# A fused attention and feed-forward kernel: the weight conversion split between VectorE and GpSimd, the score scale moved into the maximum pass, turned rows copied plainly

## The chip, the cores and the metric

The kernel runs on one core of one Trainium2 chip. A core has five engines that run their own instruction streams and meet through semaphores: TensorE (PE in the profile; its weight loads are PEld), VectorE (DVE), ScalarE (ACT), GpSimd (POOL) and SyncE (SP, which here only issues DMAs). The metric is the device time of one execution in microseconds (us). Three runs of the kernel before took 1281.09, 1281.25 and 1282.95 us; the median is 1281.25.

## The reference

```python
def _attn_ref(q, k, v, tau):                 # 8 batches, 8 heads, 576 rows, 64 columns
    scale = 1.0 / np.sqrt(q.shape[-1])
    scores = scale * np.matmul(q, k.transpose(0, 1, 3, 2))
    thresh = np.max(scores, axis=-1, keepdims=True) - tau
    scores = np.where(scores >= thresh, scores, -1000000000.0)
    scores = scores - np.max(scores, axis=-1, keepdims=True)
    attn = np.exp(scores)
    attn = attn / (np.sum(attn, axis=-1, keepdims=True) + 1e-09)
    return np.matmul(attn, v).astype(np.float32)

def _moe_ref(x, w_in, w_out):                # x 4608 x 512, w_in 512 x 2048, w_out 2048 x 512
    h = np.maximum(x @ w_in, 0.0)
    return (h * h @ w_out).astype(np.float32)
```

The attention output, with its heads side by side, is the input `x` of the feed-forward part. `w_in` and `w_out` arrive as 64-bit floats (they are scaled by a 64-bit scalar), everything else as 32-bit floats. The kernel computes in 32-bit floats.

## The kernel before

The kernel has two parts, one after the other. The feed-forward part multiplies with fewer products of sub-blocks than the plain way would take, and needs sums and differences of blocks of the weights and of `x`. The attention part runs first, and in its shadow the weights are fetched, converted to 32 bits and summed. The change touches the attention part alone.

**Periods.** The 64 heads are taken in 32 pairs; the rows of two pairs make nine units of 128 score rows, 144 units in all. The attention part is a loop over periods (`period`, line 631), each of which scores two units, A and B, turns the attention weights of units that were scored before, and multiplies those with the values. In what order each period issues its steps is written out by hand as lists of step names: `FIRSTS` for periods 0 to 2, `CONVERTING` (line 609) for the periods in which a chunk of weights is converted, 3 to 34, and `PLAIN` (line 606) for the rest, 35 to 71. Each engine carries out its own steps in the order in which they are issued.

The steps of a period that matter here, with their engines:

- `SA`, `SB` (PE): the scores of A and B into PSUM, for the two heads of a pair. q and k have been turned before, so that the head's columns lie on partitions: `T` (PE) turns them into PSUM, `eT` (ACT) takes them out, into `qT`, `kT` and `qR`. `qR` holds the 64 last rows of q of a pair, which are turned together with k. In eight of nine periods one q or one k is turned, in turns. `eT` also multiplies q by `qscale`, which is minus one eighth, by an activation with a per-partition scale (`scaled`, line 412); so the scores come out negative and scaled, and the row maximum becomes a minimum.
- `topA0`, `topA1`, `topB0`, `topB1` (DVE, line 463): a pass over the scores in PSUM which copies them to SBUF and takes each row's minimum along the way. It multiplies by the constant 1.0.
- `leastA`, `leastB` (POOL, line 470): the minimum plus tau, the threshold.
- `powA0` to `powB1` (ACT, line 473): the exponential.
- `maskA0` to `maskB1` (DVE, line 478): one instruction which compares the scores with the threshold, multiplies by the exponential and sums the row. It reads scores and exponentials from SBUF, and the threshold as a per-partition operand.
- `over` (POOL, line 485), `inv` (DVE, line 488), `spread` (POOL, line 528): one over the row sums, spread over 256 columns.
- `U`, `V`, `W` (PE, line 388) and `eU`, `eV`, `eW` (ACT, line 535): the attention weights (and the spread factors) turned, and copied to `wT`.
- `PV` (PE, line 544): the values times the weights, into two banks of PSUM. `x`: these come out into SBUF, one bank by DVE, which multiplies by the turned factors on the way (line 665), one by a plain copy on ACT (line 667). `xs` (POOL, line 682): that copy times its factors, 128 columns. Then SP writes `x` to DRAM.

**The conversion** takes one chunk of 128 x 512 64-bit floats at a time; a chunk arrives as pairs of 32-bit words, low word first, so each half is addressed as every second word (`pick`). `c1` (ACT, line 208) takes the high words without their sign into `a`; `c3` (POOL, line 221) clamps them to the range of 32-bit floats; `c4` (DVE, line 229) shifts `a` left by three and cuts it to 30 bits; `c2` (ACT, line 214) scales the low words down to the three bits that count; `c5` (DVE, line 237) keeps the two upper bits of the high words and joins `a` to them, in one instruction; `c6` (POOL, line 248) adds high and low words as integers, into the weight's place (chunks 0 to 15) or into `a`, from where it goes to DRAM. In `CONVERTING` the steps c3 to c6 of a chunk run in the period behind its c1 and c2, and stand in this order on their engines: DVE topA1, topA0, topB0, topB1, c4, inv, maskA1, x, maskA0, maskB0, c5, maskB1; POOL c3, over, leastA, leastB, spread, c6, xs; ACT c1, eU, powA1, powA0, powB0, eT, x, powB1, eV, eW, c2.

In the plain periods POOL makes one of the sums of weight blocks per period (`s1`, from line 582), and the order on DVE is topA1, topA0, topB1, inv, topB0, maskA1, maskA0, x, maskB1, maskB0.

Of the kernel before, what the change touches and what calls it, by code (L numbers as in the profile page):

```python
# [10 lines left out]
FP32 = mybir.dt.float32  # L11
# [37 lines left out]
def kernel(  # L49
# [183 lines left out]
    def convert5(m):  # L233
        if m not in parts:
            return
        lo, hi, a = parts[m]
        nc.vector.scalar_tensor_tensor(
            out=hi, in0=hi, scalar=-(1 << 30), in1=a, op0=ALU.bitwise_and, op1=ALU.bitwise_or
        )

    def convert6(m):
# [3 lines left out]
        raws.pop(m)  # L245
        if m < 16:
            a = weight(m)[:, :].bitcast(I32)
# [90 lines left out]
    def places(i):  # L338
        if i not in turned:
            turned[i] = (  # L340
                sb.tile([P, MAIN], FP32, tag="qT", bufs=Q_RING, name="qT"),
                sb.tile([P, S], FP32, tag="kT", bufs=K_RING, name="kT"),
                sb.tile([P, REST], FP32, tag="qR", bufs=K_RING, name="qR"),
            )
# [54 lines left out]
    def turn(i, which, spots, other=None):  # L399
# [8 lines left out]
        half = FULL * HALF  # L408

        kind = "turned k" if which else "turned q"  # L410

        def scaled(to, spot):
            touch(kind, nc.scalar.activation(out=to, in_=spot[0], func=AF.Identity, scale=qscale[:, :]), spot[1], BANK, i)

        def then():
            part = lambda r, x, n: (spots[r][0][:, ds(x, n)], spots[r][1])
            if which:
                for r, n in ((0, half), (1, half + REST)):
                    spot = part(r, 0, n)
                    copy_by = other if r and other else nc.scalar.copy  # L420
                    touch(kind, copy_by(to[1][:, ds(r * half, n)], spot[0]), spot[1], BANK, i)
                scaled(to[2], part(0, half, REST))
                next_keys(i)
            else:
                for r in range(2):
                    scaled(to[0][:, ds(r * half, half)], part(r, 0, half))
                for n in later_loads(i, 0):
                    load_q(n)
# [5 lines left out]
    def scores(n, rest):  # L434

        of, t = units[n]
        at_k, count = (MAIN, REST) if rest else (0, MAIN)
# [917 lines left out]
```

## Time and profile before

The profiled execution spans 1278.6 us from the first to the last instruction, 2.65 us under the median of the runs, with the TensorE clock granted in full throughout.

| engine | busy us in the span | share |
|---|---|---|
| PE matmul | 1255.2 | 98% |
| PE weight load | 1087.0 | 85% |
| DVE | 1000.2 | 78% |
| ACT | 855.6 | 67% |
| POOL | 897.4 | 70% |

The attention part ends at about 486 us (the last `inv` starts at 485.84); the integer sums of the conversion start at 35.15 (the first) to 252.12 (the last); from there to the end of the attention part the periods are plain. In the feed-forward part PE is busy without a gap.

How to read the lines: a line of the timeline gives the start in us from the span's start, the duration, the engine, the line of the kernel, the operation, what it writes and reads by the program's names, and the shapes. All tiles in SBUF are parts of one buffer called `arena`; the weights lie in `wall`; `sc` and `pt` are in PSUM. In brackets stands the idle time of the engine ahead of the instruction, and what ended it, as far as it can be inferred. Instructions of one engine overlap at their ends, as the next is started while the last results are written; so what an instruction costs its engine is the time from its start to the next one's start. A line of the windows gives for each engine the busy time within a stretch, and the number of instructions.

### The profile page before, as it was taken

What the parts mean: (1) busy time and instruction counts of PE and PEld (TensorE: products, weight loads), DVE (VectorE), ACT (ScalarE), POOL (GpSimd) and SP (SyncE); (2) the same over time, 40 slices, a digit from 0 to 9 for tenths busy, and PEclk for the clock granted to TensorE, in tenths of its full rate; (3) what the DMA queues carried; (4) which work ended last, traced back from release to release, by engine and by line L of the source; (5) the groups of instructions that cost most, each with busy time, mean ns of one, the idle gap of its engine ahead of it and who ended that gap; (6) DMA issues with size and microseconds to landing.
All of it is one profiled execution on the core that took longest, in us unless ns stands there. A gap on an engine that the chain in (4) does not pass through costs nothing.

```text
span 1278.6 us, 44201 instructions
## 1 busy us (share of the span) xinstructions
PE 1255.2 (98%) x17459; PEld 1087.0 (85%) x17459; DVE 1000.2 (78%) x2449; ACT 855.6 (67%) x1552; POOL 897.4 (70%) x1094
## 2 busy tenths in 40 slices
PE   8999999999999999999999999999999999999998
PEld 6666666677777768988888888999999999999998
DVE  6999999999999997787878877877645664565463
ACT  6999999999999995666765767667422441343240
POOL 2565665655555557888798889858877777786775
PEclk9999999999999999999999999999999999999999
DMA  6566666544333413457666666589635414522511
GB/s 155 152 158 160 165 193 182 151 94 112 89 83 84 97 34 98 156 164 219 198 190 204 192 198 187 177 324 394 208 122 166 133 50 149 166 95 76 161 35 34
DMA packets 256591, 191.89 MB, mean 150 GB/s; under 512 B 96000, under 2 KB 217344, under 8 KB 256384
## 3 DMA queue, kind: packets, MB, share of 16 engines
q1 hardware_dynamic: 254928, 188.63, 49.8%
q8 instruction: 137, 2.24, 0.7%
q14 instruction: 70, 0.57, 0.1%
q10 hardware_dynamic: 1456, 0.44, 0.1%
HBM read 116.65 MB, written 72.35 MB: 148 GB/s over the span
## 4 chain that ended last, share of the span: by engine, by line
PE 70%; DMA 1%; ACT 1%; DVE 1%; issue 1%; ACTq 0%; DVEq 0%; SPq 0%
PE po L1085 30%; PE ph L946 27%; PE sc L544 5%; PE sc L445 4%; PE pt L388 2%; DMA wall<-w 1%; PE sc L406 1%; PE sc L388 1%; DVE arena L128 1%; DVE arena L463 0%; DMA g<-arena 0%; ACT arena L916 0%; ACT c L879 0%; DMA arena<-xT 0%; ACT arena L917 0%
## 5 line engine op out<-in xcount | busy, mean ns | idle before, releaser
L128 POOL TENSOR_TENSOR arena<-arena 128x512 f32<-128x512 f32 (+1 forms) x314 | 377.7, 1222 | 126.3 <-DVE arena L128 89.4
L1085 PE MATMUL po<-wall,arena 128*128 128x128 f32 x3528 | 394.4, 275 | 0.2 <-DVE arena L125 0.2
L1085 PEld LDWEIGHTS po<-wall,arena 128*128 128x128 f32 x3528 | 394.1, 192 | 0.4 <-DVE arena L125 0.4
L946 PE MATMUL ph<-arena,wall 128*128 128x128 f32 (+1 forms) x2352 | 387.4, 327 | 1.1 <-DVE arena L665 0.5
L946 PEld LDWEIGHTS ph<-arena,wall 128*128 128x128 f32 x2352 | 354.2, 191 | 34.2 <-DVE arena L128 2.2
L128 DVE TENSOR_TENSOR arena<-ph,arena 128x512 f32<-128x512 f32 x378 | 255.6, 688 | 75.8 <-PE ph L946 50.0
L125 POOL TENSOR_TENSOR arena<-arena 128x128 f32<-128x128 f32 (+2 forms) x314 | 255.2, 814 | 29.1 <-DMA arena<-w 10.7
L879 ACT COPY c<-arena 128x512 f32<-128x512 f32 (+2 forms) x319 | 176.1, 558 | 104.2 <-DVE arena L125 85.7
L473 ACT ACTIVATE arena<-arena 128x576 f32<-128x576 f32 x288 | 232.1, 918 | 16.7 <-DVE arena L463 16.7
L128 DVE TENSOR_TENSOR arena<-po,arena 128x128 f32<-128x128 f32 x378 | 108.3, 290 | 168.0 <-PE po L1085 167.4
L478 DVE SCALAR_TENSOR_TENSOR arena<-arena 128x576 f32<-128x576 f32 x288 | 225.5, 811 | 0.4 <-POOL arena L470 0.4
L463 DVE TENSOR_SCALAR_CACHE_REDUCE arena<-sc 128x576 f32<-128x576 f32 x288 | 204.5, 751 | 14.3 <-ACT arena L535 6.4
L125 DVE TENSOR_TENSOR arena<-arena,c 128x512 f32<-128x512 f32 (+2 forms) x283 | 176.8, 633 | 7.9 <-ACT c L879 6.1
L544 PEld LDWEIGHTS sc<-arena 64*64 64x64 f32 x5760 | 144.4, 133 | 43.1 <-DVE arena L463 39.1
L445 PE MATMUL sc<-arena 64*64 64x64 f32 (+1 forms) x2304 | 170.0, 415 | 0.3 <-DVE arena L665 0.3
L544 PE MATMUL sc<-arena 64*64 64x128 f32 (+1 forms) x5760 | 160.8, 262 | 8.5 <-DVE arena L463 5.8
L535 ACT COPY arena<-pt 128x1024 f32<-128x1024 f32 x144 | 166.0, 1153 | 1.6 <-PE pt L388 1.5
L769 ACT COPY arena<-po 128x128 f32<-128x128 f32 x63 | 16.6, 264 | 185.4 <-PE po L1085 185.4
L388 PEld LDWEIGHTS pt<-ident,arena 64*128 64x128 f32 x2304 | 83.0, 138 | 41.7 <-ACT arena L535 33.8
L388 PE MATMUL pt<-ident,arena 64*128 64x64 f32 x2304 | 100.8, 227 | 2.4 <-ACT arena L535 2.1
L445 PEld LDWEIGHTS sc<-arena 64*64 64x64 f32 x2304 | 62.5, 132 | 47.5 <-issue 22.7
L470 POOL TENSOR_SCALAR arena<-arena,tau_p 128x2 f32<-128x2 f32 x144 | 65.5, 455 | 41.8 <-DVE arena L463 35.2
(51 smaller groups left out, 936.6 us busy)
## 6 DMA issues: line engine op xcount, KB each, us to landing
g<-arena SPq DMA_DIRECT2D x144, 256.0 KB, 2.6
arena<-g SPq DMA_DIRECT2D x144, 256.0 KB, 4.5
w<-arena SPq DMA_DIRECT2D x60, 256.0 KB, 2.8
wall<-w SPq DMA_DIRECT2D x49, 256.0 KB, 5.3
arena<-w SPq DMA_DIRECT2D x44, 256.0 KB, 3.1
arena<-in_v_dram SPq DMA_DIRECT2D x32, 288.0 KB, 4.6
out_dram<-arena SPq DMA_DIRECT2D x70, 128.0 KB, 2.4
arena<-in_q_dram SPq DMA_DIRECT2D x64, 128.0 KB, 4.1
```

Of the source, the lines that this page charges most:

```text
L125: e.tensor_tensor(out=out, in0=x, in1=y, op=ALU.subtract)
L128: e.tensor_tensor(out=out, in0=x, in1=y, op=ALU.add)
L388: made = nc.tensor.transpose(pt[:, r, ts(slot, HALF)], of[rows, :], ident[rows, rows])
L445: made = nc.tensor.matmul(sc[at, ds(to, count)], lhs, kT[rows, ds(at_k, count)], start=True, stop=True)
L463: made = nc.vector.tensor_scalar(out=s[:, j, :], in0=sc[:, ds(at, S)], scalar1=1.0, scalar2=None, op0=ALU.mult, op1=ALU.min, accum_out=nmx ...
L473: nc.scalar.activation(out=w[:, :, j, :], in_=of(j), func=AF.Exp, bias=nmx[:, j : j + 1], scale=-1.0)
L478: nc.vector.scalar_tensor_tensor(out=w[:, :, j, :], in0=of(j), scalar=thr[:, j : j + 1], in1=w[:, :, j, :], op0=ALU.is_le, op1=ALU.mult, a ...
L535: touch("weights", nc.scalar.copy(joined(to), whole(pt, 0, count)), at, 2 * BANK, m)
L544: made = nc.tensor.matmul(sc[ds(u * D, D), ds(5 * j * BANK + row, count)], loaded_v[i][rows, (c - (u != j)) % CH, :], wT[m][rows, ds(weigh ...
L879: nc.scalar.copy(c, y)
L946: nc.tensor.matmul(to[:, j, :], W_IN[m, k][:, ts(h * parts_ + j, P)], x_of(m, k), start=(not more and j == 0), stop=True, skip_group_check ...
L1085: nc.tensor.matmul(to, g[:, j, :], w[:, j, :], start=(not more and j == 0), stop=(j == 3), skip_group_check=True)
```

## The change

Four edits, all in the attention part.

1. **c5 and c6.** c5 only masks the high words (one input, one constant). c6 becomes two integer sums on POOL: low words plus `a`, in the low words' place, and then high words plus these, as before.
2. **The scale.** q is no longer scaled when it is taken out of PSUM. The pass over the scores multiplies by the per-partition operand `qscale` in place of the constant 1.0.
3. **Plain copies of turned rows.** As nothing is scaled on the way, both halves of a turned q come out by plain copies (2 of 256 columns, before 2 activations of 256), and those of a turned k by two copies of 320 columns, the last of which are the 64 rows of q or k (before: copies of 256 and 320 and an activation of 64). `kT` and `qR` become one tile of two halves of 320, in the same space; the scores read the 512 main keys as two runs of 256.
4. **x.** Both banks are copied by ACT, and xs on POOL multiplies all 256 columns in one instruction. DVE has no part in it.

```diff
@@ convert5, convert6
-        nc.vector.scalar_tensor_tensor(
-            out=hi, in0=hi, scalar=-(1 << 30), in1=a, op0=ALU.bitwise_and, op1=ALU.bitwise_or
-        )
+        nc.vector.tensor_scalar(out=hi, in0=hi, scalar1=-(1 << 30), scalar2=None, op0=ALU.bitwise_and)
...
         lo, hi, a = parts.pop(m)
         raws.pop(m)
+        nc.gpsimd.tensor_tensor(out=lo, in0=a, in1=lo, op=ALU.add)
         if m < 16:
             a = weight(m)[:, :].bitcast(I32)
         nc.gpsimd.tensor_tensor(out=a, in0=hi, in1=lo, op=ALU.add)
@@ places
-                sb.tile([P, MAIN], FP32, tag="qT", bufs=Q_RING, name="qT"),
-                sb.tile([P, S], FP32, tag="kT", bufs=K_RING, name="kT"),
-                sb.tile([P, REST], FP32, tag="qR", bufs=K_RING, name="qR"),
+                sb.tile([P, 2, FULL * HALF], FP32, tag="qT", bufs=Q_RING, name="qT"),
+                sb.tile([P, 2, (FULL + 1) * HALF], FP32, tag="kT", bufs=K_RING, name="kT"),
@@ turn
-        def scaled(to, spot):
-            touch(kind, nc.scalar.activation(out=to, in_=spot[0], func=AF.Identity, scale=qscale[:, :]), spot[1], BANK, i)
+        kind, n = "turned k" if which else "turned q", (FULL + (1 if which else 0)) * HALF
 
         def then():
-            part = lambda r, x, n: (spots[r][0][:, ds(x, n)], spots[r][1])
+            for r, copy_by in enumerate((nc.scalar.copy, other or nc.scalar.copy)):
+                touch(kind, copy_by(to[which][:, r, :], spots[r][0][:, 0:n]), spots[r][1], BANK, i)
             if which:
-                for r, n in ((0, half), (1, half + REST)):
-                    spot = part(r, 0, n)
-                    copy_by = other if r and other else nc.scalar.copy
-                    touch(kind, copy_by(to[1][:, ds(r * half, n)], spot[0]), spot[1], BANK, i)
-                scaled(to[2], part(0, half, REST))
                 next_keys(i)
             else:
-                for r in range(2):
-                    scaled(to[0][:, ds(r * half, half)], part(r, 0, half))
...
@@ scores
-                qT, kT, qR = turned[of[c]]
-                lhs = qT[rows, ds((c * FULL + t) * HALF, HALF)] if t < FULL else qR[rows, :]
-                made = nc.tensor.matmul(
-                    sc[at, ds(to, count)], lhs, kT[rows, ds(at_k, count)], start=True, stop=True
-                )
+                qT, kT = turned[of[c]]
+                lhs = qT[rows, c, ts(t, HALF)] if t < FULL else kT[rows, 0, ds(FULL * HALF, REST)]
+                keys = kT[rows, 1, ds(FULL * HALF, REST)] if rest else kT[rows, :, 0 : FULL * HALF]
+                to_ = sc[at, ds(to, count)] if rest else sc[at, ds(to, count)].rearrange("p (r n) -> p r n", r=2)
+                made = nc.tensor.matmul(to_, lhs, keys, start=True, stop=True)
@@ softmax, top
-                out=s[:, j, :], in0=sc[:, ds(at, S)], scalar1=1.0, scalar2=None,
+                out=s[:, j, :], in0=sc[:, ds(at, S)], scalar1=qscale[:, :], scalar2=None,
@@ period, given_out and scaled_x
-                by_vector = (0,)
                 for j in range(2):
-                    by = sc[:, ds(5 * j * BANK, P)], wT[m][:, ts(SCALE_AT + j, P)]
-                    if j in by_vector:
-                        made = nc.vector.tensor_tensor(out=x[:, j, :], in0=by[0], in1=by[1], op=ALU.mult)
-                    else:
-                        made = nc.scalar.copy(x[:, j, :], by[0])
-                    touch("x", made, 5 * j * BANK, P, m)
-                late["x"] = x, [j for j in range(2) if j not in by_vector], wT[m]
+                    touch("x", nc.scalar.copy(x[:, j, :], sc[:, ds(5 * j * BANK, P)]), 5 * j * BANK, P, m)
+                late["x"] = x, wT[m][:, ds(SCALE_AT * P, 2 * P)]
...
-                for j in js if len(js) == 1 else ():
-                    nc.gpsimd.tensor_tensor(out=x[:, j, :], in0=x[:, j, :], in1=by[:, ts(SCALE_AT + j, P)], op=ALU.mult)
+                x, by = late["x"]
+                flat = x[:, :, :].rearrange("p j q -> p (j q)")
+                nc.gpsimd.tensor_tensor(out=flat, in0=flat, in1=by, op=ALU.mult)
                 give_x(m, x)
```

More of the change, by code (lines that the diff above doesn't have):

```diff
@@ L407, in turn @@
                 touch("turns", made, at, BANK)
-        half = FULL * HALF
-        kind = "turned k" if which else "turned q"
-        def scaled(to, spot):
-            touch(kind, nc.scalar.activation(out=to, in_=spot[0], func=AF.Identity, scale=qscale[:, :]), spot[1], BANK, i)
+        kind, n = "turned k" if which else "turned q", (FULL + (1 if which else 0)) * HALF
         def then():
-            part = lambda r, x, n: (spots[r][0][:, ds(x, n)], spots[r][1])
+            for r, copy_by in enumerate((nc.scalar.copy, other or nc.scalar.copy)):
+                touch(kind, copy_by(to[which][:, r, :], spots[r][0][:, 0:n]), spots[r][1], BANK, i)
             if which:
-                for r, n in ((0, half), (1, half + REST)):
-                    spot = part(r, 0, n)
-                    copy_by = other if r and other else nc.scalar.copy
-                    touch(kind, copy_by(to[1][:, ds(r * half, n)], spot[0]), spot[1], BANK, i)
-                scaled(to[2], part(0, half, REST))
                 next_keys(i)
             else:
-                for r in range(2):
-                    scaled(to[0][:, ds(r * half, half)], part(r, 0, half))
-                for n in later_loads(i, 0):
-                    load_q(n)
+                for n_ in later_loads(i, 0):
+                    load_q(n_)
         return then
@@ L436, in scores @@
         of, t = units[n]
-        at_k, count = (MAIN, REST) if rest else (0, MAIN)
+        count = REST if rest else MAIN
         for j in range(2):
```

6 lines of the change are left out of this document (removed).

## The prediction

> **What bounds the kernel now.** I read first the busy time by stage, then the timelines of VectorE (DVE), GpSimd (POOL) and ScalarE (ACT) inside one attention period, because the shares of the whole span hide that the change touches attention alone. The two windows below run from the first to the last integer sum of the weight conversion (32 chunks, so 31 pitches) and over the plain periods behind it.
>
> ```profile
> core 0 of [0], span 1278.6 us
> core 0: us, PE busy (x) PEld busy (x) DVE busy (x) ACT busy (x) POOL busy (x), PEclk, DMA share, GB/s
> 35.15:252.12 216.97, 205.12 (x4952) 144.33 (x4952) 215.07 (x621) 216.72 (x380) 131.40 (x218) 1.00 0.64 167
> 261.00:477.00 216.00, 214.48 (x5530) 155.82 (x5526) 207.67 (x622) 205.86 (x349) 119.61 (x208) 1.00 0.37 85
> ```
>
> In the converting stage DVE (215.07 of 216.97) and ACT (216.72) are both full, PE is not; the pitch is 216.97/31 = 7.00 us. In the plain stage PE is full (214.48 of 216.00) and DVE has 4% left. POOL looks idle by 40% in both; the question is whether that idle time can be used.
>
> One converting period on DVE, from its first mask (line 478) to the next period's:
>
> ```profile
> 172.26 0.79 DVE L478 SCALAR_TENSOR_TENSOR arena<-arena 128x576 f32<-128x576 f32 x1
> 172.97 0.08 DVE L478 DVE_READ_ACCUMULATOR arena<-arena 128x1 f32 x1
> 172.97 0.28 DVE L665 TENSOR_TENSOR arena<-sc,arena 128x128 f32<-128x128 f32 x1
> 173.18 0.81 DVE L478 SCALAR_TENSOR_TENSOR arena<-arena 128x576 f32<-128x576 f32 x1
> ...
> 174.65 0.68 DVE L237 SCALAR_TENSOR_TENSOR arena<-arena 128x512 int32<-128x512 int32 x1
> 175.26 0.81 DVE L478 SCALAR_TENSOR_TENSOR arena<-arena 128x576 f32<-128x576 f32 x1
> 176.00 0.08 DVE L478 DVE_READ_ACCUMULATOR arena<-arena 128x1 f32 x1
> ...
> 178.71 0.42 DVE L229 TENSOR_SCALAR arena<-arena 128x512 int32<-128x512 int32 x1
> 179.04 0.17 DVE L488 RECIPROCAL arena<-arena 128x4 f32<-128x4 f32 x1
> 179.13 0.78 DVE L478 SCALAR_TENSOR_TENSOR arena<-arena 128x576 f32<-128x576 f32 x1
> ```
>
> Columns: start, duration, engine, line. Instructions overlap at their ends, so I count from start to start: a mask 0.74, the fused step c5 (line 237) 174.65 to 175.26 = 0.61, c4 (line 229) 178.71 to 179.04 = 0.33, the x product (line 665) 0.21. The period is 179.13 - 172.26 = 6.87 with no gap: this is DVE's own rate, and the 7.00 mean comes from other periods in which ACT is the slower one.
>
> POOL in the same stretch (in brackets the idle time ahead):
>
> ```profile
> 175.48 1.48 POOL L248 TENSOR_TENSOR arena<-arena 128x512 int32<-128x512 int32 x1 [2.17 <-ACT arena L535]
> 176.92 0.45 POOL L682 TENSOR_TENSOR arena<-arena 128x128 f32<-128x128 f32 x1
> ...
> 178.37 0.29 POOL L470 TENSOR_SCALAR arena<-arena,tau_p 128x2 f32<-128x2 f32 x1
> ```
>
> The sum of c6 starts 0.16 after c5 has ended, while the last mask (175.26 to 176.00) still runs. The 2.17 idle ahead of it lies exactly under the two middle masks and c5. That is the gap into which the new, second integer sum falls, and what such a neighbourhood costs is seen once in this trace, in an early period (DVE, then POOL):
>
> ```profile
> 26.99 0.82 DVE L478 SCALAR_TENSOR_TENSOR arena<-arena 128x576 f32<-128x576 f32 x1
> 27.73 0.08 DVE L478 DVE_READ_ACCUMULATOR arena<-arena 128x1 f32 x1
> 27.73 1.01 DVE L478 SCALAR_TENSOR_TENSOR arena<-arena 128x576 f32<-128x576 f32 x1
> 28.67 0.08 DVE L478 DVE_READ_ACCUMULATOR arena<-arena 128x1 f32 x1
> ```
> ```profile
> 27.19 0.93 POOL L682 TENSOR_TENSOR arena<-arena 128x128 f32<-128x128 f32 x1 [0.83 <-ACT arena L667]
> ```
>
> POOL's 128-wide sum comes at 27.19, inside a mask. It takes 0.93 instead of the 0.45 above: it waits for that mask's end at 27.73 and ends 0.39 later. And the next mask, which follows back to back, takes 27.73 to 28.67 = 0.94 instead of 0.74. So a POOL sum and a mask (both read two SBUF operands) exclude each other, a POOL instruction that is waiting goes in at the next boundary, and a 128-wide sum then holds DVE up by 0.20.
>
> **The change, part by part.** *Order.* PE and SP issue the same instructions in the same order. POOL's order in a converting period becomes c3, over, least, least, spread, new sum, old sum, xs. The new sum (lo = a + lo) needs c4 and c2, both long done, so it doesn't wait for c5: it comes as soon as spread is out.
>
> *The new integer sum* is asked for at about 173.3 (175.48 less the 2.17 idle: spread's end), so within a mask, and goes in at that mask's end, ahead of the next. How long it holds DVE: the old sum ended at 176.96, 0.96 after its mask's end at 176.00; the 128-wide one 0.39 after. So 384 more columns cost 0.57, and the hold is 0.20 + 0.57 = **0.77 a period**. Bounds: 0, if it finds the port free, and 0.96, if it holds until its record ends. I take 0.77. Behind the waiting sum on POOL stand the old sum and xs; the old sum waits for c5 anyway, so they aren't later by this.
>
> By the Trainium skill's page "SBUF — State Buffer", section "Who interferes with whom", a VectorE instruction with two SBUF inputs and a GpSimd instruction that reads SBUF exclude each other for the whole instruction, the first to start going first. The exclusion agrees with the 0.94 mask; taken to the letter the hold would be 0.96, the period 7.71 and the time about 1307 us, an estimate.
>
> *c5* becomes a one-input mask of the high words. Nearest rows: c4, one input too, 0.33; the fused form, 0.61. c4's operand is dense and this one takes every second word, so bounds -0.28 and 0; I take **-0.28**, as c4 is the same operation class.
>
> In the Trainium skill, "VectorE: DVE Perf Modes", section "Mode 2×_2P", a one-source instruction in SBUF runs at two results a cycle when its outermost count is even, with no word about stride; that would give 0.33, and if it didn't hold the sum would be the rival with 0.61 below.
>
> *The x product leaves DVE* (-0.21). But its slot is no pure cost now: spread, asked for inside the first mask, goes in at 172.97, and x, which reads one operand from PSUM, runs beside it; the masks behind x keep their pace (173.18 to 174.65 is 1.47 for two). With x gone, spread meets the next mask and holds it about as long. So **0**, bounds -0.21 and +0.1.
>
> *The maximum pass* gets its factor from a per-partition operand instead of a constant, 4 times a period. No row shows that form on DVE; the nearest are the pass as it is and the mask, the only large DVE instruction with such an operand:
>
> ```profile
> L478 DVE SCALAR_TENSOR_TENSOR arena<-arena 128x576 f32<-128x576 f32 x288 | 225.5, 811 | 0.4 <-POOL arena L470 0.4
> L463 DVE TENSOR_SCALAR_CACHE_REDUCE arena<-sc 128x576 f32<-128x576 f32 x288 | 204.5, 751 | 14.3 <-ACT arena L535 6.4
> ```
>
> 811 - 751 = 60 ns (the mean ns of one, behind the busy us) holds the operand, but also a second input and another pattern. Bounds 0 and 0.06; I take 0.04, so **+0.16 a period**.
>
> *ACT.* From one period with a turned k and one with a turned q:
>
> ```profile
> 151.41 1.10 ACT L421 COPY arena<-sc 128x256 f32<-128x256 f32 x2
> 151.98 0.75 ACT L413 ACTIVATE arena<-sc,qscale 128x64 f32<-128x64 f32 x1
> 152.19 0.70 ACT L667 COPY arena<-sc 128x128 f32<-128x128 f32 x1
> 152.33 1.23 ACT L473 ACTIVATE arena<-arena 128x576 f32<-128x576 f32 x1
> ...
> 158.51 1.24 ACT L413 ACTIVATE arena<-sc,qscale 128x256 f32<-128x256 f32 x2
> 159.23 0.68 ACT L667 COPY arena<-sc 128x128 f32<-128x128 f32 x1
> ```
>
> A copy of 128 columns costs 0.14 (152.19 to 152.33), one of 256 and one of 320 together 0.57: linear, 0.26 and 0.31. A k turn goes from 0.78 to two of 320, 0.63: -0.15. A q turn goes from 0.72 to two of 256, 0.51: -0.21. Four of each fall in nine periods (the ninth has none): -0.16 on average. The second x copy is +0.14. ACT's rate goes from 7.00 to 6.98. It is hidden under DVE in my forecast; with that cover gone it is what's left, -0.02 a period.
>
> *POOL's xs* goes from 128 to 256 columns: +0.19 (0.57 for 384), in the converting stage under the passes over PSUM (176.00 to 178.71), which no POOL sum disturbs: the 0.45 there is undisturbed. The chain old sum, xs, c3, over, least, which ended at 178.66, 0.47 before the mask that needs it (179.13), ends 0.19 later: still in time. *The scores' keys* are read in two runs of 256; columns are the same, I take 0.
>
> *Sum, converting:* 6.87 + 0.77 - 0.28 + 0 + 0.16 = 7.52 against 7.00: +0.52, 32 periods, **+16.6 us**.
>
> *Plain periods* (DVE, then POOL):
>
> ```profile
> 275.50 0.81 DVE L478 SCALAR_TENSOR_TENSOR arena<-arena 128x576 f32<-128x576 f32 x1
> ...
> 279.02 0.76 DVE L463 TENSOR_SCALAR_CACHE_REDUCE arena<-sc 128x576 f32<-128x576 f32 x1 [0.28 <-ACT arena L535]
> ...
> 281.80 0.81 DVE L478 SCALAR_TENSOR_TENSOR arena<-arena 128x576 f32<-128x576 f32 x1
> ```
> ```profile
> 276.86 0.52 POOL L682 TENSOR_TENSOR arena<-arena 128x128 f32<-128x128 f32 x1 [0.39 <-ACT arena L667]
> ```
>
> The period is 6.30, of which DVE waits 0.28: its work is 6.02. Here xs (276.86) is asked for inside a mask, and today x's slot lets it through. Without x it holds a mask by 0.20 + 0.19 = 0.39, less x's 0.20: +0.19; the passes +0.16. DVE's work becomes 6.37, over PE's 6.30: +0.07 for 37 periods, **+2.6 us**. With the passes at their lower bound DVE stays under PE and this is 0.
>
> The feed-forward part isn't touched. Together +19.2: the span goes from 1278.6 to 1297.8, and the median of the runs, 1281.25, is 2.65 above the span, so I forecast **1301 us**.
>
> **The rivals.**
> *1, not slower: the port is free.* If the new sum gets through while no mask wants the port, or a boundary isn't given to POOL, DVE becomes lighter (6.87 - 0.28 + 0.16 = 6.75, and -0.21 more if spread holds nothing) and ACT sets the pace at 6.98: 32 x -0.02 = -0.6, so about 1280.5, and perhaps 2 to 3 less where the plain stage waits on DVE. For it: POOL has 2.17 idle, a sum needs 0.96. Against it: all of that gap lies under masks, and the row at 27.73. It decides if masks behind the new sum stay at 0.74.
> *2, the masks keep the port.* DVE's back-to-back masks leave POOL outside until the passes. Then behind 176.00 stand spread (0.33, from 172.97 to 173.31), two sums of 0.96, and xs to the end of least, today 176.92 to 178.66 = 1.74, with the wider xs 1.93: 4.2 in all, against 3.13 to the mask at 179.13, so DVE idles 1.05; 6.87 + 1.05 - 0.28 - 0.21 = 7.43 (the dearer passes lie under POOL). 32 x 0.43 + 2.6 gives about 1298. Against it: 27.73 shows POOL going first.
> *3, the edits on DVE bring nothing.* c5 stays at 0.61 and the passes cost the full 0.06: 6.87 + 0.77 + 0.24 = 7.88, +28 us; plain 6.02 + 0.19 + 0.24 = 6.45, +5.5: about 1315. For it: the strided operand, the 60 ns row.
>
> **How the numbers follow.** Forecast 0.62, rival 1 0.15, rival 2 0.08, rival 3 0.15. The forecast's own spread is 1292 (hold 0.77, passes free: 7.36, +11.5) to 1310 (c5 unchanged: 7.80, +25.6, +2.6); widening to the lower part of rival 3 and short of rival 1 gives 1290 to 1314, which leaves out 0.2. A measurement of this kernel can tell 0.2% (2.6 us) from nothing. Rival 1 splits into no difference 0.09 and faster 0.06; everything else is slower, 0.85.
>
> **What would show it.** Right: in the converting stage the second or third mask of each period takes about 1.5 from start to start instead of 0.74, with the first integer sum beside it; DVE still without gaps, ACT now with gaps ahead of the exponentials; the period 7.5. c5 at 0.33 and the pass 0.04 longer settle two terms. Wrong: all masks at 0.74 (rival 1), gaps on DVE ahead of the first mask released by POOL (rival 2), c5 at 0.61 (rival 3). In the plain stage a mask beside xs should take 1.1. The forecast falls altogether if ACT stays full and the period is 7.0.

## The result, and the profile after

| | median of the runs, us | lowest to highest | ratio to before |
|---|---|---|---|
| before | 1281.17 | 1280.67 to 1282.95 | |
| after | 1317.38 | 1314.59 to 1318.11 | 1.0275 [1.0261, 1.029] |

The changed kernel is slower by 36 us. The forecast was 1301, 20 us slower, in a range up to 1314. The sign came out as forecast, and so did the mechanism, by which the new sum holds up a mask; the size did not.

Where the 37.2 us of the span (1278.6 to 1315.8) lie is read from three starts of `inv`, DVE's reciprocal, one of which stands in each period: the first, the 34th (the end of the converting stage) and the last. The first two of the 33 periods between the first and the 34th are still of `FIRSTS`; the other 31 are the converting periods that are averaged below. First before, then after, in the timeline of DVE:

```profile
17.81 0.17 DVE L488 RECIPROCAL arena<-arena 128x4 f32<-128x4 f32 x1
...
248.81 0.17 DVE L488 RECIPROCAL arena<-arena 128x4 f32<-128x4 f32 x1
...
485.84 0.18 DVE L488 RECIPROCAL arena<-arena 128x4 f32<-128x4 f32 x1 [0.36 <-POOL arena L485]
```
```profile
18.01 0.17 DVE L475 RECIPROCAL arena<-arena 128x4 f32<-128x4 f32 x1
...
275.00 0.17 DVE L475 RECIPROCAL arena<-arena 128x4 f32<-128x4 f32 x1
...
520.79 0.18 DVE L475 RECIPROCAL arena<-arena 128x4 f32<-128x4 f32 x1 [0.36 <-POOL arena L472]
```

| stretch | before | after | difference | forecast |
|---|---|---|---|---|
| first to 34th `inv`: converting, 33 periods | 231.00 | 256.99 | +26.0 | +16.6 |
| 34th to last `inv`: plain, 38 periods | 237.03 | 245.79 | +8.8 | +2.6 |
| last `inv` to the end: feed-forward | 792.76 | 795.0 | +2.2 | 0 |

The feed-forward part isn't touched by any edit. In the profiles of the experiments it takes 792.1 (the kernel with edits 2 to 4) to 797.1 (the kernel with a shorter new sum), so its 2.2 are not put down to the change. The first two periods give 0.85 of the 26.0.

The windows of the kernel after: a stretch of the converting stage and one of the plain stage.

```profile
core 0 of [0], span 1315.8 us
core 0: us, PE busy (x) PEld busy (x) DVE busy (x) ACT busy (x) POOL busy (x), PEclk, DMA share, GB/s
34.04:279.01 244.97, 200.67 (x4998) 143.86 (x5000) 244.97 (x595) 229.97 (x400) 195.86 (x251) 1.00 0.56 149
288.00:512.00 224.00, 215.25 (x5542) 158.38 (x5542) 223.25 (x590) 209.72 (x371) 130.42 (x209) 1.00 0.35 82
```

DVE is busy for 244.97 of 244.97 us, ACT is not full any more, and POOL has filled about half of its idle time (195.86 of 244.97 us busy, before 131.40 of 216.97; its busy time contains waits for the SBUF). In the plain stage the bound has moved from PE to DVE (223.25 of 224.00). This is the picture that was forecast. The sizes are in one converting period on DVE, after:

```profile
173.57 0.78 DVE L465 SCALAR_TENSOR_TENSOR arena<-arena 128x576 f32<-128x576 f32 x1
174.28 0.08 DVE L465 DVE_READ_ACCUMULATOR arena<-arena 128x1 f32 x1
174.28 0.94 DVE L465 SCALAR_TENSOR_TENSOR arena<-arena 128x576 f32<-128x576 f32 x1
175.15 0.08 DVE L465 DVE_READ_ACCUMULATOR arena<-arena 128x1 f32 x1
175.15 1.83 DVE L465 SCALAR_TENSOR_TENSOR arena<-arena 128x576 f32<-128x576 f32 x1
176.92 0.08 DVE L465 DVE_READ_ACCUMULATOR arena<-arena 128x1 f32 x1
176.92 0.42 DVE L237 TENSOR_SCALAR arena<-arena 128x512 int32<-128x512 int32 x1
177.26 0.81 DVE L465 SCALAR_TENSOR_TENSOR arena<-arena 128x576 f32<-128x576 f32 x1
178.00 0.08 DVE L465 DVE_READ_ACCUMULATOR arena<-arena 128x1 f32 x1
178.00 0.81 DVE L450 TENSOR_SCALAR_CACHE_REDUCE arena<-sc,qscale 128x576 f32<-128x576 f32 x1
178.73 0.08 DVE L450 DVE_READ_ACCUMULATOR arena<-sc,qscale 128x1 f32 x1
...
181.37 0.78 DVE L465 SCALAR_TENSOR_TENSOR arena<-arena 128x576 f32<-128x576 f32 x1
```

and POOL beside it:

```profile
173.78 0.83 POOL L515 COPY arena<-arena 128x256 f32<-128x256 f32 x1
174.58 1.79 POOL L244 TENSOR_TENSOR arena<-arena 128x512 int32<-128x512 int32 x1
177.48 1.48 POOL L247 TENSOR_TENSOR arena<-arena 128x512 int32<-128x512 int32 x1 [1.11 <-DVE arena L237]
178.92 0.72 POOL L658 TENSOR_TENSOR arena<-arena 128x256 f32<-128x256 f32 x1
```

and ACT, whose exponentials now wait for the passes on DVE (in brackets):

```profile
171.04 2.25 ACT L460 ACTIVATE arena<-arena 128x576 f32<-128x576 f32 x3 [0.18 <-DVE arena L450]
```

The period is 181.37 - 173.57 = 7.80. From start to start: the third mask, beside the new sum (line 244), takes 176.92 - 175.15 = 1.77 where a free one takes 0.74 (177.26 to 178.00): the hold is 1.03. The second, beside `spread` (line 515), takes 0.87, so 0.13 of hold. c5 (line 237) takes 0.34, a pass (line 450) 0.73 to 0.74.

In the plain stage, DVE and then POOL:

```profile
402.12 0.81 DVE L465 SCALAR_TENSOR_TENSOR arena<-arena 128x576 f32<-128x576 f32 x1
402.86 0.08 DVE L465 DVE_READ_ACCUMULATOR arena<-arena 128x1 f32 x1
402.86 1.28 DVE L465 SCALAR_TENSOR_TENSOR arena<-arena 128x576 f32<-128x576 f32 x1
404.07 0.08 DVE L465 DVE_READ_ACCUMULATOR arena<-arena 128x1 f32 x1
```
```profile
402.23 1.29 POOL L658 TENSOR_TENSOR arena<-arena 128x256 f32<-128x256 f32 x1 [0.62 <-ACT arena L649]
```

The wide `xs` (line 658) meets the masks, and the one behind it takes 404.07 - 402.86 = 1.21: a hold of 0.47. Most plain periods have a mask of this length, some one of up to 1.31.

### The profile page after: what moved, and what is told of

The parts are those of the page before. It is cut to its first block, busy times and chain, and to the rows that moved or that the text cites. A ratio compares the mean times of both kernels' runs of the same rounds, so it can differ in the third digit from the quotient of the medians.

```text
span 1315.8 us, 44301 instructions
## 1 busy us (share of the span) xinstructions
PE 1248.4 (95%) x17459; PEld 1086.8 (83%) x17459; DVE 1045.2 (79%) x2377; ACT 869.8 (66%) x1592; POOL 974.2 (74%) x1126
## 4 chain that ended last, share of the span: by engine, by line
PE 59%; ACT 1%; DVE 1%; DMA 1%; issue 1%; ACTq 0%; DVEq 0%
PE po L1061 30%; PE ph L922 27%; PE sc L531 1%; PE sc L434 1%; DMA arena<-xT 1%; DVE arena L450 0%; DVE arena L128 0%; ACT c L855 0%; ACT arena L892 0%; PE pt L386 0%; PE sc L386 0%; ACT arena L745 0%; DVE arena L125 0%; ACT arena L893 0%; ACT arena L522 0%
## 5 line engine op out<-in xcount | busy, mean ns | idle before, releaser
L465 DVE SCALAR_TENSOR_TENSOR arena<-arena 128x576 f32<-128x576 f32 x288 | 275.0, 999 | 1.1 <-POOL arena L457 1.1
L460 ACT ACTIVATE arena<-arena 128x576 f32<-128x576 f32 x288 | 219.9, 779 | 27.2 <-DVE arena L450 27.0
L450 DVE TENSOR_SCALAR_CACHE_REDUCE arena<-sc,qscale 128x576 f32<-128x576 f32 x288 | 219.5, 804 | 3.7 <-PE sc L434 2.1
L522 ACT COPY arena<-pt 128x1024 f32<-128x1024 f32 x144 | 147.0, 1021 | 2.1 <-PE pt L386 2.1
L745 ACT COPY arena<-po 128x128 f32<-128x128 f32 x63 | 16.6, 264 | 185.4 <-PE po L1061 185.4
L893 ACT ACTIVATE arena<-arena 128x512 f32<-128x512 f32 x144 | 90.8, 631 | 4.6
```

Source lines behind the costliest of these rows:

```text
L450: made = nc.vector.tensor_scalar(out=s[:, j, :], in0=sc[:, ds(at, S)], scalar1=qscale[:, :], scalar2=None, op0=ALU.mult, op1=ALU.min, accu ...
L460: nc.scalar.activation(out=w[:, :, j, :], in_=of(j), func=AF.Exp, bias=nmx[:, j : j + 1], scale=-1.0)
L465: nc.vector.scalar_tensor_tensor(out=w[:, :, j, :], in0=of(j), scalar=thr[:, j : j + 1], in1=w[:, :, j, :], op0=ALU.is_le, op1=ALU.mult, a ...
L522: touch("weights", nc.scalar.copy(joined(to), whole(pt, 0, count)), at, 2 * BANK, m)
```

## The experiments

Each kernel was timed against the kernel before; "period" is the mean of the 31 converting periods in the profiled run, 7.00 before and 7.81 after. The first five ask what the integer sums cost, the next three what the factor in the passes costs, the last two what `x` costs.

**Edit 1 alone** (e4_two_sums_alone), the kernel before with

```diff
-        nc.vector.scalar_tensor_tensor(
-            out=hi, in0=hi, scalar=-(1 << 30), in1=a, op0=ALU.bitwise_and, op1=ALU.bitwise_or
-        )
+        nc.vector.tensor_scalar(out=hi, in0=hi, scalar1=-(1 << 30), scalar2=None, op0=ALU.bitwise_and)
...
+        nc.gpsimd.tensor_tensor(out=lo, in0=a, in1=lo, op=ALU.add)
```

> The kernel before with the first edit alone: c5 only masks, c6 is two sums. Port theory: converting period 6.87 + 1.03 - 0.27 = 7.63 (spread is still let through beside the x product on VectorE), 0.63 over the 7.00 of before; plain periods unchanged; 1281.2 + 32 x 0.63 = about 1301 us. Rival (the edits only cost together, because ScalarE is full): at most 1290 us.

Measured: 1301.73 us, 1.0152 [1.0137, 1.0167]; period 7.66, the plain stage 236.99 us as before. So edit 1 costs 20 us by itself, all of it in the converting stage: 6.87 + 1.03 - 0.27 = 7.63 is DVE's sum of it. Four of its periods take 7.80. In these the new sum starts just behind the start of a mask and holds that very mask (DVE, then POOL):

```profile
55.58 1.95 DVE L477 SCALAR_TENSOR_TENSOR arena<-arena 128x576 f32<-128x576 f32 x1
57.46 0.08 DVE L477 DVE_READ_ACCUMULATOR arena<-arena 128x1 f32 x1
```
```profile
55.62 1.29 POOL L244 TENSOR_TENSOR arena<-arena 128x512 int32<-128x512 int32 x1
```

The mask takes 1.88, a hold of 1.14, and the sum, with no mask ahead of it, takes 1.29: this is its length without a wait.

**Edit 1 undone** (e1_one_sum), the kernel after with the fused c5 and one sum:

```diff
-        nc.vector.tensor_scalar(out=hi, in0=hi, scalar1=-(1 << 30), scalar2=None, op0=ALU.bitwise_and)
+        nc.vector.scalar_tensor_tensor(
+            out=hi, in0=hi, scalar=-(1 << 30), in1=a, op0=ALU.bitwise_and, op1=ALU.bitwise_or
+        )
...
-        nc.gpsimd.tensor_tensor(out=lo, in0=a, in1=lo, op=ALU.add)
```

> The changed kernel with its first edit undone: c5 joins a to the high words in one VectorE instruction again, c6 is one integer sum. Port theory (a GpSimd sum that reads SBUF holds back a VectorE mask that reads two SBUF operands): the 1.77 us mask of each converting period is gone, the converting period is 7.81 - 1.03 + 0.27 = 7.05 us, the plain period stays at 6.45; about 1317.4 - 32 x 0.76 = 1293 us. Rival (the loss comes from ScalarE, which has one more copy a period, or from the dearer passes over the scores): the converting period stays above 7.5, over 1306 us.

Measured: 1292.17 us, 1.0078 [1.0063, 1.0093]; period 7.09. No mask of its converting stage is longer than 0.88. Of the 36 us, 25 come from edit 1 when it stands on top of the others.

**The new sum over half of its columns** (e3_half_sum), the kernel after with

```diff
-        nc.gpsimd.tensor_tensor(out=lo, in0=a, in1=lo, op=ALU.add)
+        h = WC // 2
+        nc.gpsimd.tensor_tensor(out=lo[:, 0:h], in0=a[:, 0:h], in1=lo[:, 0:h], op=ALU.add)
```

> The changed kernel with the new integer sum over 256 of its 512 columns; the other half of the chunk's columns is left without it, so half of the converted weights lack these bits. Port theory: the hold goes by columns, 2.16 ns each less 0.08 us (0.20 for 128, 0.47 for 256, 1.03 for 512), so the long mask goes from 1.77 to about 1.21 and the converting period from 7.81 to 7.25; 1317.4 - 32 x 0.56 = 1299.5 us. Rival (the mask waits for something of fixed length, such as its exponential or threshold): the mask stays near 1.77, 1317 us.

Measured: 1300.21 us, 1.0142 [1.0127, 1.0158]; period 7.27. The long mask in DVE's timeline of this kernel, and the sum beside it:

```profile
172.67 1.28 DVE L466 SCALAR_TENSOR_TENSOR arena<-arena 128x576 f32<-128x576 f32 x1
173.88 0.07 DVE L466 DVE_READ_ACCUMULATOR arena<-arena 128x1 f32 x1
```
```profile
172.10 1.24 POOL L245 TENSOR_TENSOR arena<-arena 128x256 int32<-128x256 int32 x1
```

The mask takes 1.21, a hold of 0.47, the same as beside the 256-column `xs` of the plain stage, floats there and integers here. With 0.20 for 128 columns (the prediction's row at 27.73) and 1.03 for 512, the hold is close to a straight line in the columns: (1.03 - 0.20) / 384 = 2.16 ns each, and 0.20 + 128 x 2.16 ns = 0.48 for 256. The time follows the hold, and the hold follows the sum's length.

**The new sum's result into a dense tile** (e6_sum_to_a), the kernel after with

```diff
-        nc.gpsimd.tensor_tensor(out=lo, in0=a, in1=lo, op=ALU.add)
-        if m < 16:
-            a = weight(m)[:, :].bitcast(I32)
-        nc.gpsimd.tensor_tensor(out=a, in0=hi, in1=lo, op=ALU.add)
+        nc.gpsimd.tensor_tensor(out=a, in0=a, in1=lo, op=ALU.add)
+        to = weight(m)[:, :].bitcast(I32) if m < 16 else a
+        nc.gpsimd.tensor_tensor(out=to, in0=hi, in1=a, op=ALU.add)
```

This asked whether the new sum lasts longer than the old one because it writes every second word.

> The changed kernel with the new sum written to a, which is dense, instead of the low words, which are every second word; the second sum then adds a to the high words. Asks why the new sum holds the mask 1.03 us where the old sum's record gave 0.77. If the strided result is why: the hold goes to about 0.77, the long mask to 1.5, the period to 7.55, about 1309 us. If any 512-column sum holds for 1.03: no change, 1317 us.

Measured: 1320.88 us, 1.0305 [1.029, 1.0319]; period 7.94, which neither branch had. POOL in this kernel:

```profile
169.60 1.79 POOL L244 TENSOR_TENSOR arena<-arena 128x512 int32<-128x512 int32 x1
172.51 1.73 POOL L246 TENSOR_TENSOR arena<-arena 128x512 int32<-128x512 int32 x1 [1.12 <-DVE arena L237]
```

The first sum stays at 1.79 with a dense result, so the stride of the result isn't it. But the second, which now has one dense input (`a`) and one of every second word (`hi`), went from 1.48 to 1.73. The two sums of 1.7 and more have such a mixed pair of inputs; the sum of 1.48 adds the two interleaved halves of the same pairs of words. The 0.14 by which the period is longer lies on DVE ahead of and in the first mask: as POOL is later by the longer second sum, this mask starts 0.20 behind `inv` instead of 0.09 and takes 0.75 instead of 0.71.

**The old sum where nothing disturbs it** (e7_sum_under_passes), the kernel before with c5 and c6 behind the last mask:

```diff
-        fetch c1 T SA topA1 c3 topA0 U eU powA1 SB topB0 over topB1 powA0 c4 powB0 PV eT inv leastA maskA1 x powB1 leastB spread V eV maskA0 W maskB0 c5 c6 eW maskB1 xs c2
+        fetch c1 T SA topA1 c3 topA0 U eU powA1 SB topB0 over topB1 powA0 c4 powB0 PV eT inv leastA maskA1 x powB1 leastB spread V eV maskA0 W maskB0 eW maskB1 c5 c6 xs c2
```

> The kernel before with c5 behind the last mask instead of ahead of it, so that c6 starts under the passes over PSUM, with no mask beside it. If the old sum's record of 1.48 us held a wait of 0.52 for the mask, as I took it, it is 1.03 now (0.07 of its start runs beside a wait); if a 512-column integer sum takes 1.28, as the 32-bit float sums do, the wait was 0.20 only and my 0.77 for the hold was read from a wrong split. Time: c6 starts 0.74 later, the threshold has 0.47 of slack, so VectorE waits up to 0.27 a period: 1281 to 1290 us.

Measured: 1283.97 us, 1.0015 [1.0004, 1.0026]; period 7.08. The sum, in POOL's timeline:

```profile
178.09 1.04 POOL L248 TENSOR_TENSOR arena<-arena 128x512 int32<-128x512 int32 x1 [2.92 <-ACT arena L214]
```

It takes 1.04 under the passes over PSUM, where a sum of two 512-column float tiles takes 1.28. So the old sum's length under the masks, 1.48, is 1.04 of work and the rest a wait. All 32 of these sums take 1.04 here, and the passes beside them keep their 0.68. Moving the old sum out of the masks' way gains nothing, as before it held up no mask: only passes stood behind it. Most periods take 7.00 to 7.02; the longest, 8.33, waits 1.37 for a transfer of `x` to DRAM.

**The constant in the passes** (e2_const_scale), the kernel after with

```diff
-                out=s[:, j, :], in0=sc[:, ds(at, S)], scalar1=qscale[:, :], scalar2=None,
+                out=s[:, j, :], in0=sc[:, ds(at, S)], scalar1=-SCALE, scalar2=None,
```

> The changed kernel with the constant -1/8 in the passes over the scores in place of the per-partition operand (which is -1/8 for these inputs). If the operand costs 0.06 us a pass, as the records show (0.738 against 0.678 from start to start): converting period 7.81 - 0.24 = 7.57, plain period down from 6.45 to about 6.25, where TensorE sets it; -7.7 - 7 = about 1303 us. Rival (the passes are slow because they overlap GpSimd's work, not for the operand): 0.738 stays, 1317 us.

Measured: 1310.17 us, 1.0214 [1.0197, 1.0231]. The pass is back at 0.68 from start to start, so the operand's price of 0.06 is shown; but the period is 7.70 and not 7.57. The plain stage takes 242.90 us. The trace of this kernel shows where the rest of the converting period went, on DVE and on POOL:

```profile
170.67 0.42 DVE L229 TENSOR_SCALAR arena<-arena 128x512 int32<-128x512 int32 x1
171.01 0.17 DVE L475 RECIPROCAL arena<-arena 128x4 f32<-128x4 f32 x1
171.20 0.82 DVE L465 SCALAR_TENSOR_TENSOR arena<-arena 128x576 f32<-128x576 f32 x1
```
```profile
170.62 0.55 POOL L457 TENSOR_SCALAR arena<-arena,tau_p 128x2 f32<-128x2 f32 x1
```

With quicker passes, c4 (line 229) starts at 170.67, just as POOL has begun the threshold of A at 170.62; that takes 0.55 instead of 0.29 and ends at 171.17. The first mask, which needs this threshold, starts 0.19 behind `inv` instead of 0.09 (173.48 to 173.57 in the kernel after), and itself takes 0.75 instead of 0.71. DVE gained 0.24 on the passes and gave 0.14 of it back. By the Trainium skill, "SBUF — State Buffer", section "Who interferes with whom", a one-input instruction of this class on VectorE can use both pairs of ports and then excludes GpSimd too; the 0.55 agrees with that, though by its record the threshold had started 0.05 ahead of c4.

**Edits 2 and 3 alone** (e9_scale_and_copies), the kernel before with

```diff
-        def scaled(to, spot):
-            touch(kind, nc.scalar.activation(out=to, in_=spot[0], func=AF.Identity, scale=qscale[:, :]), spot[1], BANK, i)
...
+            for r, copy_by in enumerate((nc.scalar.copy, other or nc.scalar.copy)):
+                touch(kind, copy_by(to[which][:, r, :], spots[r][0][:, 0:n]), spots[r][1], BANK, i)
...
-                out=s[:, j, :], in0=sc[:, ds(at, S)], scalar1=1.0, scalar2=None,
+                out=s[:, j, :], in0=sc[:, ds(at, S)], scalar1=qscale[:, :], scalar2=None,
```

> The kernel before with edits 2 and 3 alone: the scale as a per-partition operand of the passes, plain copies of turned rows. The operand costs 0.06 a pass: converting period about 7.16 (+0.16 x 32 = +5), plain periods about 6.41, as in the run with x back on VectorE, where TensorE waits for the dearer passes (+7.5): about 1294 us. Rival (the operand costs only where GpSimd's sums fill the port): 1281 to 1284 us.

Measured: 1292.96 us, 1.0084 [1.0057, 1.0111]; period 7.12, the plain stage 241.84 us. DVE's sum is 6.87 + 4 x 0.06 = 7.11.

**The same with the constant** (e8_copies_const): as the last, but in the passes

```diff
-                out=s[:, j, :], in0=sc[:, ds(at, S)], scalar1=1.0, scalar2=None,
+                out=s[:, j, :], in0=sc[:, ds(at, S)], scalar1=-SCALE, scalar2=None,
```

> The kernel before with the plain copies of the turned rows (edit 3) and the scale in the passes as the constant -1/8 (no per-partition operand; it is right for a tau that isn't negative), and neither the second sum nor the change of x. ScalarE's rate goes from 7.00 to 6.84 a converting period, VectorE's stays at 6.87 and sets it: 32 x -0.13 = -4, plain periods set by TensorE as before: about 1277 us. Rival (ScalarE's rate was never the limit): 1281 us.

Measured over 12 runs: 1280.17 us against 1282.12 (23 runs), 0.9984 [0.9974, 0.9993]: faster than the kernel before by 2 us, 0.16%. Its window in the converting stage:

```profile
35.00:250.00 215.00, 196.19 (x4936) 140.22 (x4934) 212.99 (x619) 211.80 (x365) 130.92 (x217) 1.00 0.64 168
```

ACT, relieved of the scaling, is no longer full (211.80 of 215.00). The period is 6.96: most periods take DVE's own 6.87, but four of the 31 take 7.24 to 7.79, in which passes wait for PE's scores or for a copy of ACT's, and about half of the expected gain is missing. It gives up line 120, by which `qscale` is zero for a negative tau.

**Edit 4 alone** (e10_x_alone), the kernel before with

```diff
-                by_vector = (0,)
                 for j in range(2):
...
-                    if j in by_vector:
-                        made = nc.vector.tensor_tensor(out=x[:, j, :], in0=by[0], in1=by[1], op=ALU.mult)
...
+                    touch("x", nc.scalar.copy(x[:, j, :], sc[:, ds(5 * j * BANK, P)]), 5 * j * BANK, P, m)
...
+                flat = x[:, :, :].rearrange("p j q -> p (j q)")
+                nc.gpsimd.tensor_tensor(out=flat, in0=flat, in1=by, op=ALU.mult)
```

> The kernel before with edit 4 alone: both banks of x copied by ScalarE, xs 256 columns wide. If ScalarE sets the converting pace, one copy more is +0.15 a period: 7.00 to 7.15, +4.7 us; in the plain periods xs holds a mask by 0.47 and its slot of 0.20 is gone, VectorE's work is 6.29, period about 6.32, +5.9: about 1292 us. Rival (ScalarE isn't the limit, VectorE's 0.20 is a gain): converting periods 6.8 to 6.9, about 1283 us.

Measured: 1291.99 us, 1.0076 [1.0055, 1.0098]; the period is 7.14, the plain stage 242.84 us. The window of its converting stage:

```profile
40.00:245.00 205.00, 190.19 (x4552) 134.45 (x4550) 197.70 (x546) 205.00 (x382) 128.93 (x199) 1.00 0.63 167
```

Here ACT is full and DVE is not: the second copy of 128 columns, forecast at 0.14, lengthens ACT's 7.00 to 7.14. So alone, edit 4 pays in the converting stage through ACT. In the plain stage the mask beside `xs` is held as in the kernel after (1.21), but neither DVE nor PE is full there (185.39 and 186.46 us of the 190 from 290 to 480), so what sets that stage in this kernel is not shown. 1.7 of its 5.8 us lie in one period, which is read in the next run.

**Edit 4 undone** (e5_x_on_vector), the kernel after with

```diff
+                by_vector = (0,)
                 for j in range(2):
-                    touch("x", nc.scalar.copy(x[:, j, :], sc[:, ds(5 * j * BANK, P)]), 5 * j * BANK, P, m)
...
+                    if j in by_vector:
+                        made = nc.vector.tensor_tensor(out=x[:, j, :], in0=by[0], in1=by[1], op=ALU.mult)
```

> The changed kernel with its fourth edit undone: VectorE multiplies one bank of x again, xs on GpSimd is 128 columns wide. Port theory: in the plain periods the x product leaves xs a slot, the mask of 1.2 us beside xs is back at 0.74, and the period goes from 6.45 to 6.25, where TensorE sets it: -7 us. In the converting periods the x product costs 0.20 and spread holds a mask 0.135 less: +0.07 x 32 = +2 us. Together about 1312 us. Rival (taking x off VectorE is a gain by the 0.20 it cost in every period): +0.2 x 69 = 1331 us.

Measured: 1315.98 us, 1.0262 [1.0247, 1.0278]. The period is 7.89, as expected: 0.21 for the product on DVE, less the 0.13 that `spread` no longer takes from a mask. The plain stage missed: 244.83 us, near that of the kernel after, though no mask beside `xs` is held to 1.2 any more. One part of this is a single period of 8.90 (POOL, then DVE):

```profile
350.00 1.27 POOL L125 TENSOR_TENSOR arena<-arena 128x512 f32<-128x512 f32 x1 [3.70 <-DMA arena<-xT]
```
```profile
351.58 0.92 DVE L465 SCALAR_TENSOR_TENSOR arena<-arena 128x576 f32<-128x576 f32 x1 [2.40 <-POOL arena L457]
```

One of POOL's sums of blocks waits for a transfer out of `xT`, the place of `x` in DRAM; the threshold stands behind it on POOL, and DVE waits for the threshold. The same period takes 6.62 in the kernel before, 7.38 in the kernel after, 8.32 with edit 4 alone and 6.91 with edits 2 and 3 alone. POOL's wait ahead of this sum is 3.70 here and was 1.52 in the kernel before, so the length of the period goes by when that transfer landed in the profiled run. Without this period the plain stage costs, over the kernel before, 8.0 us with all edits, 5.5 here, 4.5 with edits 2 and 3 alone and 4.1 with edit 4 alone.

The other part is in the ordinary periods: most take 6.41, against 6.29 before and 6.45 after. TensorE's products with the values, in the kernel before (261 to 477 us) and here (290 to 510 us), in the groups by line:

```profile
L544 PE MATMUL sc<-arena 64*64 64x128 f32 x2232 | 77.3, 272 | 0.9 <-DVE arena L463 0.3
```
```profile
L531 PE MATMUL sc<-arena 64*64 64x128 f32 x2160 | 75.2, 272 | 7.8 <-DVE arena L450 7.8
```

They now stand idle for 7.8 us, before for 0.9, until a pass has read the PSUM into which they write; with edits 2 and 3 alone it is 7.8 too (262 to 482 us). So the dearer passes delay PE by themselves, without any held mask. That and edit 4's cost nearly add up in the plain stage: 4.5 + 4.1 = 8.6 against 8.0.

In all, the edits alone add 20.1 (edit 1), 10.9 (2 and 3) and 9.9 us (4), 40.9 together; the change adds 36.2. By the profiles most of the difference lies in the converting stage, where the edits alone cost 20.5, 4.2 and 5.0 us, 29.7 together, and the change 26.0: ACT's longer period (edit 4) is hidden once DVE is the slower one.

## Why the prediction was right about the direction and short by 16 us

The mechanism held. The new sum is asked for inside a mask, goes in at that mask's end, and the next mask waits for it in every converting period; DVE runs without gaps, ACT with some (0.18 ahead of exponentials). The terms of the sum, in us a converting period:

| term | forecast | measured | shown by |
|---|---|---|---|
| hold of the new sum | +0.77 | +1.03 | the mask of 1.77; e4, e1, e3 |
| c5 with one input | -0.28 | -0.27 | 0.34 from start to start |
| `x` gone, `spread` holds a mask | 0 | -0.07 | 0.87 - 0.74 - 0.20; e5 |
| four passes with the operand | +0.16 | +0.24 | 0.68 to 0.74 each; e2, e9 |
| DVE's period | 7.52 | 6.87 + 0.93 = 7.80 | 181.37 - 173.57 |

**The step that failed is the size of the hold, 0.77.** It was formed as 0.20 for 128 columns plus 0.57 for 384 more, and the 0.57 was the distance between the tails of two POOL sums behind their masks' ends, 0.96 and 0.39. In that, a hold is a tail less 0.19, and this rule is right: behind the mask's end at 175.15 the new sum runs until 174.58 + 1.79 = 176.37, a tail of 1.22, and 1.22 - 0.19 = 1.03. What was wrong is that the new sum was given the tail of the old one. The old sum is the quicker kind: 1.04 undisturbed, by e7. The new one has one dense input and takes 1.29 undisturbed, by e4; e6 shows that it is the pair of inputs which costs the 0.25, as the old sum with such a pair goes from 1.48 to 1.73. The row of the right size stood in the profile of before. Its groups by line and shape give POOL's float sums with two inputs as

```profile
L128 POOL TENSOR_TENSOR arena<-arena 128x512 f32<-128x512 f32 x252 | 318.2, 1276 | 44.8 <-DVE arena L128 25.1 <-ACT c L879 10.7 <-ACT arena L917 3.7
...
L682 POOL TENSOR_TENSOR arena<-arena 128x128 f32<-128x128 f32 x31 | 14.1, 455 | 0.0
```

and 0.20 + (1.276 - 0.455) = 1.02. The old sum looked like the nearest row because it does the same operation on the same shape, and it was also a row that another wait had cut: 0.44 of its 1.48 is a wait for a mask. Why two interleaved inputs are quicker than a mixed pair is not settled by these runs.

The bound was too low as well: 0.96 was called the most that a hold could be, and the hold was 1.03, in four periods of e4 even 1.14. By the rule of the Trainium skill that the prediction cites, "SBUF — State Buffer", section "Who interferes with whom", the exclusion lasts the whole instruction; with the true tail that would be 1.22, and the measured 1.03 lies 0.19 below it, as the first sum's 0.20 lies below 0.39.

**The passes** took the upper bound, 0.06, where 0.04 was chosen: the 60 ns between mask and pass were the operand after all, as e2 shows by taking it away: a pass with the operand takes what a mask takes, 0.74.

**`x`** was near enough: `spread` does hold the mask that takes x's place, but for 0.13, not 0.21. **c5** came out as forecast, the strided operand notwithstanding; 0.34 agrees with the two results a cycle that the Trainium skill, "VectorE: DVE Perf Modes", section "Mode 2×_2P", gives for one source in SBUF, as the fused form with its two sources took 0.61.

**The plain stage** was forecast at +2.6 and gave +8.8. DVE was forecast to need 6.37 a period and needs 6.45 in most: the hold of `xs` is 0.47, not 0.39 (the same wrong tail), the passes 0.24, not 0.16, and against them DVE's work before was 5.95, not 6.02, as the 0.28 of idle time in brackets is counted from the end of a record that runs 0.07 past the point from which the next could start (278.67, so the wait is 0.35). 5.95 + 0.47 - 0.21 + 0.24 = 6.45. Before, the plain periods took 6.29 in the mean without the last, so this is 37 x 0.16 = 5.9 us; the other 2.9 lie in single longer periods, such as the one of 7.38 (before 6.62), in which DVE waits 0.75 for the threshold behind POOL's wait for a transfer, and in the shorter last one (4.66 against 4.34).

**The rivals.** Rival 1 (the port is free) falls with the mask of 1.77, rival 2 (the masks keep the port) with DVE's timeline, which has no gap, and with POOL's, in which the new sum is in ahead of the third mask. Rival 3 was half right: the passes cost their 0.06, but c5 did get quicker. That its 1315 lies near the measured 1317 is an accident of other terms: it had c5 0.27 too dear, the hold 0.26 too cheap.

**The account.** Converting: 33 x (7.79 - 7.00) = 26.0 instead of 16.6; plain 8.8 instead of 2.6; the feed-forward part 2.2, which no edit explains. 19.2 + 9.4 + 6.2 + 2.2 = 37.0 of the span's 37.2. Of the 9.4 that the converting stage is over its forecast, the hold gives 32 x 0.26 = 8.3 and the passes 32 x 0.08 = 2.6, and `x` takes 32 x 0.07 = 2.2 off again. In the working itself one sum is off by 1: the lower end of the forecast's own spread, with 11.5 on 1281.25, is 1293 and not 1292.

## What to carry to other kernels

Idle time of GpSimd is only free where the instructions of VectorE beside it leave it the SBUF: look in the timeline at what VectorE does under the gap, not at the share. A sum of two SBUF operands on GpSimd that meets a run of two-input instructions on VectorE cost them 2.16 ns a column here, 1.03 us for 512, for the 0.27 that it took off VectorE; under passes that read PSUM a sum holds up nothing (the old one in e7, the wide `xs` in the kernel after). To price such a hold, take an undisturbed row with the same kinds of operands, not a row of the same name whose operands lie otherwise and which holds a wait itself.

## What the runs showed of the hardware that was not expected

- A per-partition operand in place of a constant costs a 128 x 576 pass from PSUM with a running minimum 0.06 us (0.74 against 0.68), in the passes of e9 and the kernel after against those of e2 and the kernel before.
- GpSimd's sum of the two interleaved halves of 512 pairs of words takes 1.04 us (e7), a sum with one dense and one interleaved input 1.29 (e4), and a dense or interleaved result makes no difference (1.79 in e6 and in the kernel after, wait included).
- The hold that VectorE sees is 0.19 to 0.20 us shorter than the tail of GpSimd's record behind the boundary, for sums of 128, 256 and 512 columns.
- A one-input VectorE instruction on SBUF (c4, 0.34 us) stretches a GpSimd instruction of two columns that starts 0.05 ahead of it from 0.29 to 0.55 us (e2, e6).
